# The tail of one V tile as sixteen eight-row loads in a decode kernel of four attention layers

## The chip, the cores and the metric

The kernel runs on one core of a Trainium2 chip. The metric is the device time of one execution in microseconds, the median of the runs. The core has five instruction streams that matter here (TensorE, VectorE, ScalarE, GpSimd, and SyncE, which only issues loads) and sixteen DMA engines that move the bytes from the chip's main memory (HBM) into the on-chip buffer (SBUF, 128 partitions).

## What is computed

One token goes through four attention layers. Layers 0 and 2 use the weights and caches A, layers 1 and 3 those of B. Each layer normalises the vector, projects it to 32 heads of 192, takes the scores against 8192 cached keys per head, the softmax, the weighted sum of 8192 cached values, and the output projection.

```python
def _A_ref(x, k_cache, v_cache, wq, wo):
    q = (x @ wq).reshape(B, Sq, 32, 192).transpose(0, 2, 1, 3)
    scores = jnp.einsum("bhqd,bhkd->bhqk", q, k_cache) * (192 ** -0.5)
    p = _softmax(scores, axis=-1)
    o = jnp.einsum("bhqk,bhkd->bhqd", p, v_cache)
    return o.transpose(0, 2, 1, 3).reshape(B, Sq, 32 * 192) @ wo

x = x + _A_ref(_layernorm(x), A_k_cache, A_v_cache, A_wq, A_wo)
x = x + _B_ref(_layernorm(x), B_k_cache, B_v_cache, B_wq, B_wo)
x = x + _A_ref(_layernorm(x), A_k_cache, A_v_cache, A_wq, A_wo)
x = x + _B_ref(_layernorm(x), B_k_cache, B_v_cache, B_wq, B_wo)
```

`x` is 640 wide, everything is bf16. The caches are the bulk: 32 heads x 8192 positions x 192 numbers x 2 bytes is 100.7 MB for K, as much for V, and each layer reads both.

## The kernel before

The heads are taken in sixteen pairs. A pair's K (or V) is one tile of 6144 KB: 128 partitions, 64 for each head, with 48 KB in each partition. SBUF has a pool of eight slots of 24 KB per partition (`TS` = 12288 numbers is one slot). A whole tile takes two neighbouring slots and is loaded by one transfer (line 379); where two neighbouring slots are not free together, it is loaded in two halves (line 381).

For a pair p of layer l the steps are: VectorE multiplies the K tile by the query (`products`, line 599), TensorE sums the products into scores, the softmax follows, and TensorE multiplies the V tile by the probabilities (`values`, line 678 and the helper at line 58), with one wait for each half of the tile. `gather` brings the result into a row. Fifteen rows of pairs later, in three groups, the output projection uses them.

All loads are issued by SyncE in one order, `plan`, written out at lines 226 to 281: in layer 0 each pair adds its K, then its V, with the output weights (`wo`) in between at three places. `allot` chooses the slots, `freed` holds for each load the event after which its slot may be overwritten. The function `transfer` issues one load: it waits for the events in `free`, starts the DMA and gives the slot's semaphore `semS[i]`, with an increment of 16 when the load has landed. `need` gives the event to wait for, and `ahead` issues loads in the order of the plan as far as their slots have a release that is known. Since SyncE works in order, a load that waits for its slot holds back all that come behind it.

Queue.op counts the increments of each semaphore in program order and returns the pair of semaphore and value to wait for. So a wait for the last of several transfers on one semaphore is a wait for all of them.

The tile V6 (pair 6) is loaded whole in layer 0 and in layer 2, with K7 as the next load in the plan: whole in layer 0 and in two halves in layer 2. The lines in question in `transfer`:

```python
if whole(*n[:3]):
    if n[3] == 1:
        return landed[n[:3] + (0,)]
    f = lambda s: s.dma_start(pool[:, i * TS:(i + 2) * TS], r)
```

Here `r` is the tile in HBM as 128 rows of 48 KB, `i` the first of the two slots.

## Time and profile before

| | |
|---|---|
| median of three runs | 1982.24 us (1981.79 to 1982.29) |
| span of the profiled execution | 1982.1 us |
| TensorE busy | 1288.6 us (65%) |
| VectorE busy | 1201.2 us (61%) |
| read from HBM | 848.36 MB, 428 GB/s over the span |
| DMA packets | 26930 |
| chain that ended last | DMA 67%, VectorE 17%, TensorE 15%, ScalarE 1% |

The profile shows one execution. The busy time of an engine is the time in which it worked; the chain that ended last is followed back from the last instruction, at each step to what released it. A load appears twice: as SyncE's short issue, and in the chain from its issue to the arrival of its last byte. In the median, a whole tile lands 37.9 us after its issue for B's K, 36.4 for A's K, 33.5 for B's V and 27.5 for A's V; most of that is waiting behind earlier loads in the queue.

By stretch, the DMA engines' share and rate are 1.00 and 432 GB/s from 190 to 1000 us, 0.96 and 388 GB/s from 1003 to 1030 us, where layer 1 ends and layer 2 begins, and 1.00 and 430 GB/s from 1030 to 1970 us.

### The profile page before, as it was taken

What the parts mean: (1) busy time and instruction counts of PE and PEld (TensorE: products, weight loads), DVE (VectorE), ACT (ScalarE), POOL (GpSimd) and SP (SyncE); (2) the same over time, 40 slices, a digit from 0 to 9 for tenths busy, and PEclk for the clock granted to TensorE, in tenths of its full rate; (3) what the DMA queues carried; (4) which work ended last, traced back from release to release, by engine and by line L of the source; (5) the groups of instructions that cost most, each with busy time, mean ns of one, the idle gap of its engine ahead of it and who ended that gap; (6) DMA issues with size and microseconds to landing.
All of it is one profiled execution on the core that took longest, in us unless ns stands there. A gap on an engine that the chain in (4) does not pass through costs nothing.

```text
span 1982.1 us, 13748 instructions
## 1 busy us (share of the span) xinstructions
PE 1288.6 (65%) x8248; PEld 146.4 (7%) x3160; DVE 1201.2 (61%) x1376; ACT 139.9 (7%) x462; POOL 4.5 (0%) x23
## 2 busy tenths in 40 slices
PE   3567476666466666666785676675776766657658
PEld 0001001000100100100020010010001001000001
DVE  3566467467166657556745565665764775665656
ACT  0000000000000000000010000000000100000000
POOL 0000000000000000000000000000000000000000
PEclk9787776778677777777887877878787888777779
DMA  9999999999999999999999999999999999999998
GB/s 414 438 431 430 431 436 432 430 430 429 435 432 433 434 430 432 429 435 433 426 407 426 425 426 426 432 430 431 434 429 427 435 431 433 433 432 431 433 433 367
DMA packets 26930, 849.25 MB, mean 428 GB/s; under 512 B 3058, under 2 KB 3188, under 8 KB 3828
## 3 DMA queue, kind: packets, MB, share of 16 engines
q1 hardware_dynamic: 26724, 848.38, 99.6%
q8 instruction: 45, 0.74, 0.2%
q14 instruction: 17, 0.14, 0.0%
q10 hardware_dynamic: 144, 0.00, 0.0%
HBM read 848.36 MB, written 0.00 MB: 428 GB/s over the span
## 4 chain that ended last, share of the span: by engine, by line
DMA 67%; DVE 17%; PE 15%; ACT 1%; issue 0%; SPq 0%
DMA pool<-in_B_k_cache_dram 27%; DMA pool<-in_A_v_cache_dram 20%; DVE pool L599 15%; DMA pool<-in_A_k_cache_dram 14%; PE S L58 6%; DMA pool<-in_B_v_cache_dram 6%; PE OY L58 5%; PE OY L678 3%; DVE acc L697 1%; ACT p_sb L636 1%; DVE s_sb L621 1%; PE S L612 0%; DVE m_bf L623 0%; PE OY L538 0%; PE QM L626 0%
## 5 line engine op out<-in xcount | busy, mean ns | idle before, releaser
L599 DVE TENSOR_TENSOR pool<-pool,q_sb 128x3072 bf16<-128x3072 bf16 x512 | 861.1, 1753 | 229.5 <-DMA pool<-in_B_k_cache_dram 133.5
L58 PE MATMUL S<-pool,ident 128*128 128x512 bf16 x2944 | 789.5, 425 | 19.5 <-DVE pool L599 17.6
L710 PE MATMUL TB<-acc,small 128*1 128x192 f32 x240 | 82.7, 495 | 212.0 <-DVE acc L697 212.0
L58 PE MATMUL OY<-pool,p_sb 128*16 128x512 bf16 x1920 | 202.7, 498 | 0.0
L696 DVE TENSOR_SCALAR acc<-OY,small 128x192 f32<-128x192 f32 x64 | 26.7, 418 | 287.5 <-PE OY L58 256.3
L678 PE MATMUL OY<-pool,p_sb 128*16 128x512 bf16 (+1 forms) x1216 | 148.2, 495 | 69.5 <-DMA pool<-in_A_v_cache_dram 63.5
L612 PE MATMUL S<-pool,ident 128*128 128x512 bf16 x128 | 61.8, 483 | 201.3 <-DVE pool L599 201.2
L697 DVE SCALAR_TENSOR_TENSOR acc<-OY,small,acc 128x192 f32<-128x192 f32 x424 | 177.1, 418 | 14.9
L621 DVE TENSOR_REDUCE s_sb<-S 128x64 f32<-128x512 f32 x128 | 88.0, 688 | 69.7 <-PE S L58 69.7
L527 ACT ACTIVATE q_sb<-QM 128x192 bf16<-128x192 f32 x60 | 19.9, 331 | 944.0 <-PE QM L521 944.0
L721 ACT ACTIVATE rows<-TB,small 1x192 bf16<-1x192 f32 x120 | 43.2, 406 | 596.3 <-PE TB L710 596.3
L692 DVE RECIPROCAL small<-TB 1x2 f32<-1x2 f32 x64 | 11.2, 175 | 94.5 <-PE TB L651 75.3
L636 ACT ACTIVATE p_sb<-s_sb,small 64x128 bf16<-64x128 f32 x128 | 55.7, 435 | 161.2 <-DVE small L630 160.4
L612 PEld LDWEIGHTS S<-pool,ident 128*128 128x128 bf16 x128 | 12.9, 101 | 676.2 <-DVE pool L599 604.4
L651 PE MATMUL TB<-small,ones 128*1 128x2 f32 x120 | 11.4, 165 | 74.1 <-ACT p_sb L636 74.1
L678 PEld LDWEIGHTS OY<-pool,p_sb 128*16 128x16 bf16 (+1 forms) x1216 | 39.8, 107 | 217.3 <-issue 138.8
L626 PE MATMUL QM<-ident,m_bf 128*64 128x64 bf16 x128 | 14.0, 216 | 54.4 <-DVE m_bf L623 53.9
L710 PEld LDWEIGHTS TB<-acc,small 128*1 128x1 f32 x240 | 19.8, 101 | 310.8 <-DVE acc L697 284.0
L630 DVE TENSOR_REDUCE small<-QM 128x1 f32<-128x64 f32 x64 | 14.4, 225 | 35.2 <-PE QM L626 35.2
L521 PEld LDWEIGHTS QM<-rows,one_b 1*64 1x64 bf16 x120 | 6.2, 100 | 347.0 <-issue 341.1
L538 PE MATMUL OY<-oT,pool 128*128 128x1 bf16 x675 | 28.6, 178 | 1.9 <-ACT oT L584 1.9
L538 PEld LDWEIGHTS OY<-oT,pool 128*128 128x128 bf16 x675 | 27.8, 131 | 3.8 <-ACT oT L584 2.5
(74 smaller groups left out, 215.2 us busy)
## 6 DMA issues: line engine op xcount, KB each, us to landing
pool<-in_B_k_cache_dram SPq DMA_DIRECT2D x28, 6144.0 KB, 37.9
pool<-in_B_v_cache_dram SPq DMA_DIRECT2D x28, 6144.0 KB, 33.5
pool<-in_A_v_cache_dram SPq DMA_DIRECT2D x27, 6144.0 KB, 27.5
pool<-in_A_k_cache_dram SPq DMA_DIRECT2D x34, 3072.0 KB, 20.5
pool<-in_A_k_cache_dram SPq DMA_DIRECT2D x14, 6144.0 KB, 36.4
pool<-in_A_v_cache_dram SPq DMA_DIRECT2D x10, 3072.0 KB, 14.7
pool<-in_B_k_cache_dram SPq DMA_DIRECT2D x8, 3072.0 KB, 22.5
pool<-in_A_wo_dram SPq DMA_DIRECT2D x6, 2400.0 KB, 21.9
```

Source lines behind the costliest of these rows:

```text
L58: return t.add_instruction(mybir.InstMatmult(name=t.bass.get_next_instruction_name(), engine=mybir.EngineType.PE, ins=[t.lower_ap(rhs), t. ...
L527: lambda a: a.activation(q_sb[i][:], QM[:, 0:DH], ACT.Copy), e, last["q"][i], bank=QMu)
L538: e = PE.op(lambda t, i=i, c=c, f=y_first[0], fin=n[0] == "wol" and i == k - 1: t.matmul(YB[:, c:c + 1], lhsT=t3[:, i, c:D:DC], rhs=o[:, i ...
L599: e = DV.op(lambda v, d0=d0: v.tensor_tensor(k3[:, :, d0:d0 + QD], kin[:, :, d0:d0 + QD], q_sb[qi][:, d0:d0 + QD].unsqueeze(1).broadcast_t ...
L612: t.matmul(S[:, :], lhsT=ident[:], rhs=k3[:, :, d0:d0 + R], start=True, stop=fin) if d0 == 0 else
L621: lambda v, u=u: v.tensor_reduce(s[:, u * JU:(u + 1) * JU], SP_[u][:].rearrange("p (j r) -> p j r", r=R), AX.X, ALU.add), ev_S[p, u], last ...
L636: ev_p[p] = AC.op(lambda a, h=h, r=r: a.activation(p_sb[par][r, :, h], s[r, :], ACT.Exp, bias=negm[par][r, 0:1], accum_out=l_col[par][r, h ...
L678: t.matmul(o, lhsT=x, rhs=y, start=f, stop=fin) if c == 0 else
L696: v.tensor_scalar(acc[:], O[:, 0:DH], pick[:, 0:1], None, ALU.mult) if i == 0 else
L697: v.scalar_tensor_tensor(out=acc[:], in0=O[:, i * DH:(i + 1) * DH], scalar=pick[:, i:i + 1], in1=acc[:], op0=ALU.mult, op1=ALU.add)), e if ...
L710: e = PE.op(lambda t, h=h: t.matmul(TB[96:97, C_O + h * DH:C_O + (h + 1) * DH], lhsT=half[:, h:h + 1], rhs=acc[:], start=True, stop=True), ...
L721: last["TO"] = last["row_written"] = AC.op(lambda a, h=h: a.activation(orow[:, o0 + h * DH:o0 + (h + 1) * DH], TB[96:97, C_O + h * DH:C_O ...
```

## The change

A set `SHARED` names the two tiles: V6 of layer 0 and V6 of layer 2. For these, `transfer` issues one load of the first 42 KB of each of the 128 rows, and then sixteen loads of eight neighbouring rows each, with the last 6 KB of each row. All seventeen increment the same semaphore, by 16 each; the event that is returned is that of the last, so a wait for the tile has the count of all seventeen. Only the first waits for the slots' release.

```diff
+SHARED = (("v", 0, 6), ("v", 2, 6))
...
                     if n[3] == 1:
                         return landed[n[:3] + (0,)]
+                    if n[:3] in SHARED:
+                        x = 2 * TS - TS // 4
+                        SP.op(lambda s: s.dma_start(pool[:, i * TS:i * TS + x], r[:, 0:x]), *free, sem=semS[i], inc=16)
+                        for y in range(0, P, 8):
+                            e = SP.op(lambda s, y=y: s.dma_start(pool[y:y + 8, i * TS + x:(i + 2) * TS], r[y:y + 8, x:]),
+                                      sem=semS[i], inc=16)
+                        return e
                     f = lambda s: s.dma_start(pool[:, i * TS:(i + 2) * TS], r)
```

The order of the plan, the slots, the compute and all other loads are as before.

## The prediction

> **What bounds the kernel.** I read the page first: its span, the busy shares, the slices and the queues, then the chain.

> ```profile
> span 1982.1 us, 13748 instructions
> ...
> DMA  9999999999999999999999999999999999999998
> ...
> q1 hardware_dynamic: 26724, 848.38, 99.6%
> q8 instruction: 45, 0.74, 0.2%
> q14 instruction: 17, 0.14, 0.0%
> ```

> The slices show sixteen DMA engines busy from the first to the last one; the queue table shows that nearly all of it is q1, SyncE's queue of loads. 848 MB at 428 GB/s is the time. Compute is off this path: TensorE 65%, VectorE 61%. The sum below is made against this execution's 1982.1 us; the median of the runs is 1982.24, so 0.1 us more.

> Next the DMA issues of SyncE around the two places, from the timeline (start, duration, line). V6 of layer 0 is the load at 198.47, V6 of layer 2 the one at 1202.10.

> ```profile
> 193.34 0.33 SPq L379 DMA_DIRECT2D pool<-in_A_k_cache_dram  x1
> 198.47 0.33 SPq L379 DMA_DIRECT2D pool<-in_A_v_cache_dram  x1
> 207.77 0.33 SPq L379 DMA_DIRECT2D pool<-in_A_k_cache_dram  x1
> ```

> ```profile
> 1186.88 6.08 SPq L381 DMA_DIRECT2D pool<-in_A_k_cache_dram  x2
> 1202.10 0.33 SPq L379 DMA_DIRECT2D pool<-in_A_v_cache_dram  x1
> 1216.30 6.26 SPq L381 DMA_DIRECT2D pool<-in_A_k_cache_dram  x2
> ```

> Then the chain of work that ended last, in layer 2 around that load (start, length, what):

> ```profile
> 1202.10 26.33 DMA pool<-in_A_v_cache_dram
> 1228.43 0.04 issue
> 1228.47 0.60 PE OY L678 x3
> ...
> 1233.80 24.38 DMA pool<-in_A_v_cache_dram
> ```

> The load takes 26.33 us from issue to landing, though a 6144 KB load occupies the engines for 14.5 us (the loads of layer 0 land 14.5 us apart: 217.9, then 232.5). So it first queues for some 12 us, and TensorE starts 0.04 us after the last byte. What counts is the slowest of the sixteen engines: a load has landed when all have marked it.

> **Which engine is slowest.** The trace holds, for each load, the sixteen times at which the engines marked their shares complete. At the start all sixteen marks lie within 1.1 us. At the end of layer 1 (load whose last mark is at 1009.6) they trail the first by 0, 0.1, 0.4, 0.5, 0.6, 1.2, 1.8, 3.0, 3.6, 4.8, 5.0, 5.1, 5.6, 5.6, 5.9 and 6.4 us. At the layer border, where no load can be issued for a moment, most of this is lost; by the last load of the V tile (1978.1) it is 0 to 3.2 for eight and 4.1, 4.1, 4.5, 4.7, 5.2, 5.3, 5.4, 6.1 for the other eight. The marks step where q8 fetches 16 KB of instructions: one engine then falls back by 1.5 us, and the 45 fetches go round eight engines in turn (the fetches at 59.0, 433.6 and 780.4 us, eight apart, hit the same one). The 8 KB fetches of q14 near 86, 267, 425, 620 and 801 push a ninth engine back by 0.96 us each; it is the one at 6.4 at the end of layer 1 and near 5.2 at the end. If the change loads some engines more and others less, it moves these numbers; the latest of the sixteen in each half sets the time.

> **What the change removes.** Each of the two V6 loads shrinks from 48 to 42 KB a row. A DMA engine carries eight rows, 1.819 us each by the median packet of 49,152 bytes; 6 KB less in eight rows is 48 KB at 27.0 GB/s, so 1.8 us less on every engine.

> **What it adds on SyncE.** Sixteen issues. The closest two unhindered issues in the trace start at 145.37 and 145.74, so 0.37 us each and 5.9 us for sixteen. Behind them stands K7's issue, at 207.77 in layer 0 and 1216.30 in layer 2. Both wait for a release until then; the free time is 207.77 - 198.80 = 9.0 us and 1216.30 - 1202.43 = 13.9 us. Cost: nothing, covered by these two waits, and the DMA engines have about 12 us of work queued. Without that cover it would be 5.9 us once per tile. No semaphore wait is added: TensorE's one wait for the tile only has a higher count. No compute instruction changes.

> **What it adds on the DMA engines.** A transfer has 48 KB in eight rows of 6 KB. The trace has no eight-row load. It shows that a row is one packet on one engine, so eight rows reach at most eight engines. If these are always the same eight, each carries 16 x 6 KB = 96 KB more and the other eight nothing.

> Cheapest: bytes alone. The nearest packet, 6400 bytes, takes 0.244 us; 16 x 0.244 = 3.9, and 16 marks add about 0.1. Less the 1.8 removed, the eight fall back by 2.1 to 2.2 us (I take 2.1), the others gain 1.8.

> Dearest: no overlap at all between the sixteen. SyncE's waits show how long the smallest transfer takes by itself, two rows of the output:

> ```profile
> SPq L98 <- DMA out_dram<-pool: 1.0, 1, 1.0
> ```

> 16 x 1.0 = 16.0, less 1.8: 14.2 us a tile, 28.4 for both.

> Between these I take the row that is nearest to a small piece among large ones: the 16 KB fetch. Its bytes are worth 0.61 us, it costs its engine 1.5, so 2.5 times its bytes. 96 KB are 3.64 us, times 2.5 is 9.1, less 1.8: the eight fall back by 7.3 us per tile. It is an estimate; what eight rows that are neighbours do to each other is the unknown here.

> [...]

> **The sum.** The fall of 7.3 us adds to what those eight engines trail by already. If the ninth is among them: end of layer 1 6.4 + 7.3 against 6.4, +7.3; in the second half 5.2 + 7.3 against 6.1, +6.4; together +13.7. If they are the eight lightest: 3.0 + 7.3 against 6.4, +3.9, then 3.2 + 7.3 against 6.1, +4.4; together +8.3. The profile does not tell which, so I take the middle, +11.0: 1982.2 + 11.0 = 1993.2. Nothing hides it: the slow engines never run dry within a half, so their delay reaches the layer's end, and the compute tail behind the last load is the same.

> **Rivals.**
> Levelling, a gain: bytes alone count and the eight are the lightest. Then 6.4 falls to max(6.4 - 1.8, 3.0 + 2.1) = 5.1, so -1.3, and 6.1 to max(4.3, 5.3) = 5.3, so -0.8: 1980.1. For it: in both halves the marks split eight and eight at a gap. Against it: there are nine late engines by cause, the ninth hit by a different queue; if the eight fetch engines are one half, the ninth belongs to the other. Even a perfect levelling to the mean (3.1 and 2.9) would give 6.4 - 3.1 + 6.1 - 2.9 = 6.5 us.

> Bytes alone, wrong engines, slower: with the ninth among the eight 6.4 + 2.1 is +2.1, and 5.2 + 2.1 against 6.1 is +1.2: +3.3, 1985.5. With the fetch engines: 5.9 + 2.1 - 6.4 and + 2.1, +3.7. It decides as soon as one engine that trails by over 4.3 us is among the eight.

> Sixteen serial transfers, the dear bound: 2 x 14.2 = 28.4 less what the lighter eight absorb (up to 3.4 + 2.9): 2004 to 2010. Against it: small packets elsewhere follow each other without a gap.

> No shift: the rows of each transfer go to sixteen engines after all, or to changing ones. The bytes are the same, and 32 marks of 9 ns cost 0.3 us: 1982.5.

> **Numbers.** About 0.2% (4 us) is what a measurement tells from no change. Forecast 0.60, its own range +6 to +16.8 (1988 to 1999); levelling 0.13; bytes on the wrong engines 0.15; serial 0.06; no shift 0.06. Levelling counts as faster beyond 4 us only if it comes near the perfect one: 0.05 of its 0.13. Same holds the other 0.08, 0.06 and all but 0.01 of the 0.15: 0.28. Slower: 0.60 + 0.06 + 0.01 = 0.67. The range runs from 1979, below the levelling, to 1999, and leaves out the serial case and the best of the levelling, some 0.12 with the forecast's tail.

> **What would show it.** In the profile after: two stretches, near 216 to 240 and 1214 to 1240 us, in which the DMA share stays high but the GB/s dip, if packets are slowed; V6 landing later than 232.5 by 5 us or more, in layer 0; the first wait of VectorE for K7 (247.1) later by the same; layer 1 ending 4 to 7 us later than 1012, layer 3 8 to 14 later. Bytes alone would show 6 KB packets at 0.24 us. I am wrong if V6 lands within 2 us of before, or if SyncE's K7 issue moves by the 5.9 us and the engines run dry.

## The result, and the profile after

The kernel with the change takes 1994.63 us (median; 1993.68 to 1995.04) against 1982.26 us for the one before: a ratio of 1.0061 with a 95% interval of 1.0048 to 1.0073. That is +12.4 us, a slowdown of 0.6%. The profiled execution spans 1993.1 us, 11.0 us more than the one before.

A time and a span are not the same: in every execution for which both are on record, the time is 1.75 to 1.95 us above the span. The runs of the kernel before that were made beside the experiments span 1979.7 to 1982.7 us, and their medians are 1980.3 to 1980.6. So the profiled execution of before, with its 1982.1 us, is a long one, and 11.0 us is less than the change costs; +12.4 us is the better number.

The page of the kernel before has this rate in its slices:

```profile
GB/s 414 438 431 430 431 436 432 430 430 429 435 432 433 434 430 432 429 435 433 426 407 426 425 426 426 432 430 431 434 429 427 435 431 433 433 432 431 433 433 367
```

The page of the changed kernel (the slices give the DMA engines' busy share and their rate in forty equal parts of the span; the queue line has packets, MB and share):

```profile
span 1993.1 us, 13780 instructions
...
DMA  9999999999999999999999999999999999999998
GB/s 410 437 429 436 398 429 435 431 433 427 435 430 433 434 431 432 432 429 435 423 398 427 432 420 399 432 414 431 435 424 428 434 435 431 432 432 431 433 433 363
...
q1 hardware_dynamic: 27236, 848.38, 99.5%
```

The engines are as busy as before and move the same 848.38 MB in 512 packets more: 256 more data packets (32 loads of eight rows) and 256 more marks of completion, eight for each of these loads. But the rate falls from 431 to 398 in the fifth slice, where V6 of layer 0 lands, and from 426 to 399 in the twenty-fifth, at V6 of layer 2. (It is low in the twenty-first slice too, at the border of layers 1 and 2, as it was before. Why it is 414 in the twenty-seventh is not known.) Busy without moving bytes is the first thing to see.

SyncE's issues around V6 of layer 0, from the timeline after (start, length, what):

```profile
199.68 0.33 SPq L382 DMA_DIRECT2D pool<-in_A_v_cache_dram  x1
200.04 5.43 SPq L384 DMA_DIRECT2D pool<-in_A_v_cache_dram  x16
209.11 0.36 SPq L387 DMA_DIRECT2D pool<-in_A_k_cache_dram  x1
```

The sixteen issues take 5.43 us and end at 205.5. K7's issue still waits until 209.11 for its slot, so nothing on SyncE is late because of them. In the chain of waits, K7 is where the delay first shows (start, length, what), first before, then after:

```profile
207.77 39.31 DMA pool<-in_A_k_cache_dram
247.08 0.02 issue
247.10 1.77 DVE pool L599
```

```profile
209.11 42.84 DMA pool<-in_A_k_cache_dram
251.95 0.02 issue
251.98 10.10 DVE pool L607 x6
```

Before, K7 came from 207.77 to 247.08; now it lands at 251.95, 4.9 us later, and VectorE (line 607 is the old 599) starts then. V6 itself lands at 237.6 instead of 232.5. In layer 2 the same step appears: the K6 half ahead of V6 lands 4.9 us late, the K7 half behind it 10.9 us late. By the last load of the kernel it is 11.0.

Busy time by stretch says what the engines did meanwhile. The last two numbers of a line are the DMA share and GB/s; the first line is the kernel before, the second the change, both from 228 to 238 us, where the tail of V6 of layer 0 comes in.

```profile
228.00:238.00 10.00, 7.36 (x74) 0.71 (x22) 5.37 (x8) 1.31 (x5) 0.00 (x0) 1.00 1.02 442
```

```profile
228.00:238.00 10.00, 6.49 (x36) 0.48 (x11) 5.71 (x8) 1.31 (x5) 0.00 (x0) 0.91 1.06 297
```

With a full share the rate falls from 442 to 297 GB/s in these 10 us, 1.45 MB less, worth 3.3 us at 433 GB/s. In layer 2 the rate from 1228 to 1239 us is 265 instead of 433, again before and after:

```profile
1228.00:1239.00 11.00, 6.74 (x52) 0.88 (x20) 4.94 (x10) 0.07 (x1) 0.00 (x0) 0.66 1.01 433
```

```profile
1228.00:1239.00 11.00, 0.41 (x4) 0.19 (x4) 0.51 (x3) 0.98 (x4) 0.00 (x0) 0.57 0.97 265
```

### The profile page after: what moved, and what is told of

The parts are those of the page before. It is cut to its first block, busy times and chain, and to the rows that moved or that the text cites. A ratio compares the mean times of both kernels' runs of the same rounds, so it can differ in the third digit from the quotient of the medians.

```text
span 1993.1 us, 13780 instructions
## 1 busy us (share of the span) xinstructions
PE 1297.4 (65%) x8248; PEld 146.8 (7%) x3160; DVE 1200.8 (60%) x1376; ACT 139.8 (7%) x462; POOL 4.5 (0%) x23
## 2 busy tenths in 40 slices
DMA  9999999999999999999999999999999999999998
## 3 DMA queue, kind: packets, MB, share of 16 engines
q1 hardware_dynamic: 27236, 848.38, 99.5%
## 4 chain that ended last, share of the span: by engine, by line
DMA 67%; PE 20%; DVE 11%; ACT 1%; issue 0%; SPq 0%
DMA pool<-in_B_k_cache_dram 27%; DMA pool<-in_A_v_cache_dram 21%; DMA pool<-in_A_k_cache_dram 13%; PE S L58 10%; DVE pool L607 9%; DMA pool<-in_B_v_cache_dram 5%; PE OY L58 5%; PE OY L686 3%; DVE acc L705 1%; ACT p_sb L644 1%; DVE s_sb L629 1%; PE S L620 1%; PE OY L546 0%; DVE m_bf L631 0%; SPq L384 0%
## 5 line engine op out<-in xcount | busy, mean ns | idle before, releaser
L58 PE MATMUL OY<-pool,p_sb 128*16 128x512 bf16 x1920 | 207.1, 508 | 0.0
```

What stands on the lines that cost most here:

```text
L58: return t.add_instruction(mybir.InstMatmult(name=t.bass.get_next_instruction_name(), engine=mybir.EngineType.PE, ins=[t.lower_ap(rhs), t. ...
```

## The experiments

Three theories were set against each other; they are suppositions of mine, and no trace shows one of them by itself. A: the place of the rows counts. Engines that work on certain rows of SBUF at the same time slow each other down, and the texts below call what they then share a path; a load of all 128 rows would leave each engine a path of its own, and a small load would send engines onto paths that are in use. B: each small load or packet costs a surcharge, wherever it goes. C: only the uneven bytes count, since eight engines carry the whole tail (each small load of the change left eight marks). The medians, each beside the runs of the kernel before on the same chip:

| run | median, us | before, us | ratio (95%) |
|---|---|---|---|
| the change | 1994.63 | 1982.26 | 1.0061 [1.0048, 1.0073] |
| apart | 1993.64 | 1982.36 | 1.0057 [1.0042, 1.0072] |
| one_tail | 1982.58 | 1982.36 | 1.0001 [0.9992, 1.0011] |
| sixteen_rows | 1990.37 | 1982.36 | 1.0041 [1.0026, 1.0056] |
| layer0_only | 1989.38 | 1982.36 | 1.0036 [1.0022, 1.0051] |
| lower_only | 1983.11 | 1982.26 | 1.0004 [0.9995, 1.0014] |
| upper_only | 1989.84 | 1982.26 | 1.0036 [1.0023, 1.0049] |
| sixteen_apart | 1989.11 | 1982.26 | 1.0034 [1.0022, 1.0046] |
| eight_full | 1983.64 | 1982.26 | 1.0007 [0.9997, 1.0016] |
| no_tail | 1978.68 | 1982.16 | 0.9982 [0.9973, 0.9991] |
| double | 2009.17 | 1982.16 | 1.0138 [1.0124, 1.0152] |

And the lengths of the tail packets, from the trace's packet records (nanoseconds; a 6 KB packet that is alone takes 234):

```
run             packets per tile   mean, layer 0   mean, layer 2
the change      128 of 6 KB             415             390
apart           128 of 6 KB             347             345
one_tail        128 of 6 KB             237             237
sixteen_rows    128 of 6 KB             440             459
layer0_only     128 of 6 KB             393              -
lower_only       64 of 6 KB             235             235
upper_only       64 of 6 KB             438             435
sixteen_apart   128 of 6 KB             398             391
eight_full     1024 of 768 bytes         39              39
double          128 of 12 KB            980             814
```

**apart.** Rows four apart in place of neighbours.

```diff
-for y in range(0, P, 8):
-    ... pool[y:y + 8, i * TS + x:(i + 2) * TS], r[y:y + 8, x:]
+for y in [q + k for q in range(0, P, 32) for k in range(4)]:
+    ... pool[y:y + 29:4, i * TS + x:(i + 2) * TS], r[y:y + 29:4, x:]
```

> The sixteen tail loads again take eight rows each, but rows that stand four apart (0, 4, ..., 28, and so on), so the engines and their bytes are as in the change. Theory A (eight neighbouring rows go through few write paths of SBUF, and their engines wait for each other): the 6 KB packets for the lower 64 rows fall to 0.23 us, those for the upper 64 still share a path with the other eight engines' own stream and stay near 0.4; each tile costs some 2.7 us instead of 5 to 6, in all +5 to +6.5 us, 1987 to 1989 us. Theory B (a small load costs its engine a surcharge, wherever its rows lie): packets stay at 0.40 us on average and the time at 1993 to 1995. Theory C (only the uneven bytes count): also 1993 to 1995.

Measured +11.3 us. A's packets came as expected, B's did not: by eighths of the tail in layer 0, the packets' means are 235, 235, 235 and 239 ns for the lower 64 rows and 425, 470, 480 and 459 for the upper ones, almost the same in layer 2. But A's time was wrong: the sum of the packets fell from 6.6 to 5.6 us for an engine, yet the tile landed as late as with the change (V6 5.2 us, K7 4.8 us behind the kernel before). The packets of one engine follow each other without a gap, so they can be put in chains, one for each engine. The last engine needs 6.8 us for its sixteen packets in the change and 6.7 in apart: in the change, engines that run ahead are held up more and the last one less (its last three packets take 392, 305 and 296 ns); in apart the last engine ends on 522 and 532. The mean is not what counts, the last engine is. The time alone fits B and C as well, so the next runs had to leave the uneven bytes out.

**one_tail.** One tail load of all 128 rows.

```diff
-for y in range(0, P, 8):
-    e = SP.op(... r[y:y + 8, x:] ...)
+e = SP.op(lambda s: s.dma_start(pool[:, i * TS + x:(i + 2) * TS], r[:, x:]), sem=semS[i], inc=16)
```

> The last 6 KB of each row come in one load of all 128 rows, so the tile takes two loads and every engine has its usual bytes. A and C: 1982 to 1983 us, the marks of V6 and K7 where they were before. B: one more load per tile, at most 0.5 us each, so the same. If cutting the tile as such were the cost, 1985 us or more.

Measured +0.2 us, no change within its interval, with packets of 237 ns. Cutting the tile in two cost nothing here.

**sixteen_rows.** Neighbours again, but sixteen of them, meant to give every engine one row of each load (a load of eight rows left eight marks).

```diff
-for y in range(0, P, 8):
+for y in range(0, P, 16):
```

with sixteen rows in both slices.

> The tail comes in eight loads of sixteen neighbouring rows, one row for each engine, so all sixteen engines have their usual bytes. C (uneven bytes): 1982 to 1983 us. [...] B (surcharge per small packet): 0.41 us a packet, 8 x 0.41 - 1.8 = +1.5 us a tile, 1985 us.

Measured +8.0 us, with 440 and 459 ns a packet where one_tail had 237. Reckoned with one row for each engine, all have their usual bytes, so C alone does not explain it; B's 1985 us is too little.

**layer0_only.**

```diff
-SHARED = (("v", 0, 6), ("v", 2, 6))
+SHARED = (("v", 0, 6),)
```

> Only V6 of layer 0 is cut. If the two tiles act one by one, what layer 0 costs (its K7 landed 4.9 us later, the last load of layer 1 5.8 us later) stays to the end: +5 to +6.3 us, 1987 to 1988.6 us. If the delay of layer 0 is lost at the border of layers 1 and 2, or the second tile's cost needs the first, less than +3 us or more than +8 us.

Measured +7.0 us, a little over the range. In the landings K7 is 5.2 us late and the last load of layer 1 5.4. So layer 0's tile costs about half of the 12.4 us, and its delay is carried over the border.

**lower_only and upper_only.** The loop of apart over the lower or over the upper 64 rows alone.

```diff
-for y in [q + k for q in range(0, P, 32) for k in range(4)]:
+for y in [q + k for q in (0, 32) for k in range(4)]:      # lower_only
+for y in [q + k for q in (64, 96) for k in range(4)]:     # upper_only
```

> Eight tail loads, rows four apart, for the lower 64 rows alone; the last 6 KB of the upper 64 rows of the two tiles are not loaded, so that part of V6 is left out. The engines that serve small loads have their usual bytes in more pieces, each on its own write path; the other eight have 48 KB less. Theory A (paths are shared): nothing is shared, packets 0.235 us, 1982 to 1982.8 us. Theory B (surcharge per small load): 8 x (0.41 - 0.235) = 1.4 us a tile, 1985 us. Theory C (uneven bytes): no engine has more, 1982 to 1982.8 us.

> The same for the upper 64 rows; the last 6 KB of the lower 64 rows of the two tiles are left out. The eight serving engines again have their usual bytes (48 KB less in the large load, 48 KB in small ones), but write on the paths of the other eight, which have 48 KB less. A: packets of 0.46 us and more, 8 x 0.235 = 1.9 us a tile lost by the serving engines, the other eight slowed as well, +2.5 to +4.5 us in all, 1985 to 1987 us. B: as lower_only, 1985 us, with packets of the same length in both. C: 1982 to 1982.8 us.

Measured +0.9 us (not clear of none, and 0.3 over the range of A and C) and +7.6 us. The same number of loads of the same shape; only the rows differ. The same stretch as above, lower_only first, then upper_only:

```profile
228.00:238.00 10.00, 7.75 (x51) 0.50 (x14) 5.81 (x8) 1.31 (x5) 0.00 (x0) 0.89 1.02 440
```

```profile
228.00:238.00 10.00, 7.12 (x54) 0.66 (x18) 5.85 (x8) 1.31 (x5) 0.00 (x0) 0.94 1.01 342
```

One rival is left by argument only. The rows that are read in HBM change together with the rows that are written in SBUF, and no run parts the two. Against a limit on the reading side stands one_tail: it reads the same 6 KB of all 128 rows, at 237 ns a packet; what differs is which engine moves which row.

**sixteen_apart.** Eight loads of sixteen rows, eight apart.

```diff
-for y in range(0, P, 8):
-    ... pool[y:y + 8, ...], r[y:y + 8, x:]
+for y in range(8):
+    ... pool[y:y + 121:8, ...], r[y:y + 121:8, x:]
```

> Eight tail loads of sixteen rows that stand eight apart, one row for each engine: all sixteen engines have their usual bytes. [...] If all of sixteen_rows' cost were the number of loads or the engines falling out of step, it stays at 1989 to 1991 us.

Measured +6.9 us with a wide spread (1987.23 to 1991.44): the median lies in the range given to the number of loads or to engines out of step (1989 to 1991 us), the fastest run below it. That one was profiled, and its packets are 398 and 391 ns. So rows eight apart are a gain in the packets against the 440 and 459 ns of sixteen_rows, and how much of the gain reaches the time stays unclear. The number of loads is not the reason, since the next run has as many; engines that fall out of step may be.

**eight_full.** Eight tail loads of all rows, 768 bytes a row.

```diff
+w = TS // 32
+for y in range(x, 2 * TS, w):
+    ... pool[:, i * TS + y:i * TS + y + w], r[:, y:y + w]
```

> Eight tail loads of all 128 rows, 768 bytes a row: as many loads as sixteen_apart, each engine with its usual bytes on its own path. A: 64 packets of about 0.036 us in place of 1.8 us, at most +0.6 us a tile, 1982 to 1983.5 us. B (a surcharge for each load): 8 x 0.18 = +1.4 us a tile, 1985 us.

Measured +1.4 us, not clear of none and 0.1 over A's range, with 39 ns a packet: 64 x 0.039 = 2.5 us for what took 1.8, so 0.7 a tile, 1.4 for both. The length of the packets is enough to explain the time; the number of loads is not the cause.

**no_tail.** The tail loads are left out altogether.

> The last 6 KB of all 128 rows of the two tiles are left out, so every engine has 48 KB less in each tile. If the latest of the sixteen engines sets the time, it is 1.8 us earlier per tile: -3.6 us, 1978.7 us. Together with lower_only, where the upper eight alone had 48 KB less and nothing was gained, this says that the latest engine is among those that serve the lower rows. If relief of one tile is lost again at the layer border, -1.5 to -2 us; if another wait ends last there, no gain.

Measured -3.5 us. In the landings V6 of layer 0 and the last load of layer 1 are 1.7 to 1.8 us early, the 1.819 us of one 48 KB packet. lower_only took the same 48 KB from the other eight engines alone and gained nothing. So the engine that is last at the end of layer 1 is one of those that serve the small loads, and what this engine carries comes out in the time, one to one.

**double.** A tail of 12 KB.

```diff
-x = 2 * TS - TS // 4
+x = 2 * TS - TS // 2
```

> The tail is 12 KB a row, still in sixteen loads of eight neighbouring rows. Sharing of paths and uneven bytes both grow with the bytes: 12 KB packets of some 0.8 us on average (0.46 alone), a cost per tile of about twice the change's, +22 to +26 us, 2004 to 2008 us. A surcharge for each load, whatever its size: 16 x 0.18 as before and the bytes double: +16 us or less.

Measured +27.0 us, 2.2 times the change, a little over the range, with packets of 980 and 814 ns. The cost goes with the bytes. No run beats the kernel before while it loads everything.

## Why the prediction was right

The forecast of 1993.2 us was for +11.0; the medians say +12.4. The likeliest case won, for its own reason, but two of its terms were off and met in the middle. That the profiled executions differ by just 11.0 is chance: the one of before is long. The prediction put its span of 1982.1 beside a median time of 1982.24, two numbers that are not of one kind.

**What bounds the kernel.** Right. The sixteen engines stay full (q1 at 99.5%), a load lands with its slowest engine (of K7's sixteen marks the last stands at 251.95, and VectorE starts at 251.98), and no_tail shows that the latest engine's bytes come out one to one. The delays stand where they were looked for: V6 5.2 us later, the end of layer 1 5.8, the last load 11.0.

**What it adds on SyncE: nothing.** Right: 5.43 us of issues, covered by K7's wait.

**What it removes: 1.8 us.** Right: an undisturbed packet of 42 KB takes 1594 ns (median in layer 0) where one of 48 KB takes 1819, and 8 x 0.225 = 1.8.

**What it adds on the DMA engines.** This is the term that was mis-sized. I took 2.5 times the bytes, from the instruction fetch: 9.1 us in sixteen packets, a fall of 7.3. Measured are 128 x 0.415 / 8 = 6.6 us in layer 0 and 6.2 us in layer 2, so a fall of 4.8 and 4.4 on average. Bytes alone would have been 16 x 0.234 = 3.7; the rest is what the packets took beyond 0.234 us each. The fetch was the nearest row, but not of the same kind.

**What the other eight engines do.** Wrong, though the forecast itself does not use it: they were to gain 1.8 us, and they lost about 2. The first of the sixteen marks of K7 stands at 246.8 where it was at 244.7, because packets of 48 KB next to the tail took up to 3.6 us instead of 1.82.

**Which engines.** The prediction left open whether the eight hold the ninth engine, the one of the q14 fetches, and took the middle of +8.3 and +13.7. They do hold it, so +13.7 was the case that applied. The marks show it: right behind V6, at K7, the sixteen spread over 5.2 us instead of 2.4, and at the next 8 KB fetch of that kind (273 us) the engine that trails by 5.2 falls to 6.1. Before, the same fetch (267 us) takes an engine from 1.4 to 2.4. At V6 the ninth was thus not yet the latest, which trailed by 2.3, and some 0.9 us of its fall stays hidden until that fetch: K7 is 4.9 us late (0.3 of it was there before the tile), the loads behind the fetch 5.6 to 5.8, and the second tile adds 6.0. A fall that was too large times a share that was too small gave the right sum: that the number came so near is luck, though the mechanism was right.

**The rivals.** Levelling is refuted in this form: the eight include the engine that is latest at the end of layer 1, and relieving the other eight (lower_only) gains nothing. (The sum for a perfect levelling has a slip: the second list of marks has a mean of 3.1, not 2.9, so 6.3 and not 6.5 us.) Bytes alone on the wrong engines, +3.3 to +3.7, is too little by 9 us, because packets take 0.39 to 0.41 us on average and not 0.24. Serial transfers are refuted by packets that overlap: 6.6 us for an engine's sixteen, where the bound had 16.0. No shift is refuted by the marks.

**Paths and engines.** What the runs show is the time of a packet by its rows: in apart 235 to 239 ns for the lower 64 rows and 425 to 480 for the upper ones, and with neighbouring rows 415 and 390 on average in the change. How many rows or engines share a path, and whether a path is what they share, no run shows. The longest tail packet of the change took 553 ns, 2.4 times the 234 of one that is alone. That the engines miss each other because they trail by up to 2.4 us is argued, not shown. That small loads go to the same engines each time stands on the eight chains of lower_only.

Three things stay open. No run has the uneven bytes without the longer packets, so how the 12.4 us divide between the two is not known; longer packets without uneven bytes, as reckoned above, cost 7.6 (upper_only) and 8.0 (sixteen_rows). How the cost of the longer packets divides among the engines in sixteen_apart was not settled. And the profiled execution of before loses up to 2 us at the border of layers 1 and 2 against those of one_tail and lower_only; why was not tried.

## What to carry to other kernels

On a kernel that is full of loads, look past the busy share: a full share at a lower GB/s (1.06 at 297 instead of 1.02 at 442) was here the sign of packets that take longer than their bytes (6 KB in 415 ns instead of 234). Prefer loads of all 128 rows: here the tail cost 0.2 us as one such load and 12.4 us as sixteen of eight rows, paid for by the eight engines that carried it (4.4 to 4.8 us a tile) and by the others (about 2 us in layer 0). Before moving load from late to early engines, find out which engine is last and whether it is among those that get more.

## What the runs showed that I had not expected

The half of the rows that the tail takes matters, not the shape alone: 64 packets of 6 KB a tile cost nothing clear of noise on the lower rows and over 7 us (two tiles) on the upper ones. The engines that got none of the tail were slowed as well, by about 2 us at V6 of layer 0.
